# Projecting out the third unit by seven block products, in a fused RWKV-6 and MoE kernel

## The chip, the cores and the metric

The kernel runs on one core of a Trainium2 chip. The metric is the device time of one launch in microseconds (us). Five engines run side by side, each with its own queue of instructions that it works off in order: TensorE (matrix products; PE in the profile, PEld its weight loads), VectorE (DVE), ScalarE (ACT), GpSimd (POOL) and SyncE (SP, which issues most DMAs). They meet only through semaphores.

## What is computed

Two parts follow each other. First a linear attention with a state that decays (RWKV-6), over 4 batches, 8 heads, 768 tokens, heads of 48. Then a feed-forward layer over the 3072 tokens, from 384 to 2048 and back, in float32:

```python
for t in range(S):
    cur = np.einsum('bhd,bhe->bhde', u[None] * kt, vt)
    y[:, :, t] = np.einsum('bhd,bhde->bhe', rt, state + cur)
    state = wt[:, :, :, None] * state + np.einsum('bhd,bhe->bhde', kt, vt)
...
h = x @ w_in
sp = np.maximum(h, 0.0) + np.log1p(np.exp(-np.abs(h)))
g = h * erf(sp)
return (g @ w_out).astype(np.float32)
```

## The kernel before, in words

**Units and steps.** The 3072 tokens are cut into 12 units of 256 tokens (two batches of 128 tokens, `UNIT`), numbered from 0. Step s computes the attention of unit s. Behind it, and interleaved by hand on the same engines, step s computes the hidden layer of unit s-1 (`hidden`, eight pieces, each two rows of 128 of the 2048) and the projection back of unit s-3 (`project` or `project_fast`). `n_steps` is 12, `DIRECT` is 4. Steps 1 to 4 run `attend`, steps 5 to 11 `attend_late`. "The third unit" is unit 2, which is projected out in step 5; "the fifth step" is step 4.

**The hidden layer.** A piece (the token H) is twelve instructions on TensorE at L1097 into one of two PSUM buffers `m`, which ScalarE copies to `h` (L1106). Units 0 to 2 (below `FAST`) get their activation through `activate`: two halves of 2048 elements a partition, each a softplus (L1079), an error function (L1082) and two multiplies (L1086), called one after another by `advance`, the token A. From unit 3 on the hidden layer is cut into four chunks of 1024 elements: `softplus_chunk` (s, L1053) writes one shared stretch of `room`, `erf_chunk` (ey or ep, L1057) writes its result into a "lane" in PSUM, either the bank of `y` or the second bank of products, and `multiply_chunk` (m, L1062) multiplies `h` by it on VectorE. Softplus and error function need different tables, so ScalarE loads a table ahead of each.

**The projection.** `project` (L1114) makes the two output tiles of a unit from 32 products of 384 columns (L1129, 64 instructions, since a float32 product is two), in eight pieces (the token P), and ScalarE copies each tile out (L1138). `project_fast` (L1197) treats the product as 2 x 2 blocks and takes seven block products of 8 x 192 columns instead of eight, in Strassen's manner as Winograd arranged it; it is used from unit 3 on. Each P is one block product:

```python
product(m0[:, lo], a11, b11, True)      # then o[0] low half <- m0, L1218
product(m1[:, lo], a22, t4, True)
product(m1[:, hi], s1, t1, False)       # then o[1] <- m1, L1223
product(m0[:, lo], s2, t2, False)       # then o[0] high half <- m0, L1226
product(m1[:, hi], s4, b22, False)
product(m0[:, lo], s3, t3, False)       # then o[1] += m0 (L1232), DMA out
product(m1[:, lo], a12, b21, True)      # then o[0] += m1 (L1237), DMA out
```

It needs four sums of blocks of the activations: `blend` makes them on VectorE, tokens S1 (L1189), S2 (L1191), S3 (L1193), S4 (L1195), into `room[1]` to `room[3]` and, for S3, in place. In the later steps, blocks of `h` are first copied to a PSUM lane by ScalarE (`to_lane`, the tokens k22y, k11p, k12y, L1170). It also needs four differences of the weights (`mix_weights`, L1153): three are made on VectorE in step 3, and the last, which overwrites a block of `w_out_sb` that the plain projection still reads, on GpSimd by the token G.

**The order.** `attend` in step 4 calls `in_order` at five places, and `attend_late` calls `run_late` at seven ("front", "near", 0 to 4). Both read a string of tokens; F is the next part of the preparation of the following step's attention. Step 5 has strings of its own (`LATE[DIRECT + 1]`), steps 6 to 10 take `USUAL`. At the last two places of step 4, between the two strings, stand the transposes and the state products of the attention (L1010, L734), the update of the middle state and the next state (L1031, L1034, L1035), and the rest of step 5's preparation (L333, L589); behind the last one come the products through the state (L685), the copies of `y` and `xT` (L693, L714) and six small DMAs for xT (L720), three of them issued by ScalarE. The first place of step 5 follows the products of level 5 (L627) and VectorE's L333 and L637.

Of the kernel before, what the change touches and what calls it, by code (L numbers as in the profile page):

```python
# [16 lines left out]

P = 128
FAST = 3
EP = 64  # L20
HC = 64
NC = 2
# [17 lines left out]
DIRECT = 4  # L40
# [21 lines left out]
def kernel(  # L62
# [26 lines left out]
    SPC = NB // NJ  # L89
    assert C == P == NC * HC and HC == 1 << LOG and NE == 2 and D <= EP and NP * NE * D == DM == KT * P  # L90
    assert n_steps == SPC * n_pairs and NP == KT + 1 == 4 and NG == 2 and P // NEAR * NH == P
# [214 lines left out]
    def rows(e, n=D):  # L306
        return slice(e * EP, e * EP + n)

    both = slice(0, EP + D)

# [362 lines left out]
    def through_state(s, xT):  # L673
# [42 lines left out]
        for kk in range(KT):  # L716
            n = D // KT
            for e in range(NE):
                queue = nc.scalar if (kk, e) in by_scalar else nc.sync
                queue.dma_start(  # L720
                    out=xT[e * EP + D : (e + 1) * EP, kk, :],
                    in_=y3[e * EP + kk * n : e * EP + (kk + 1) * n, :],
                )
# [18 lines left out]
    def spread_blocks(s, pp):  # L742
# [3 lines left out]
        for e in range(NE):  # L746
            nc.tensor.matmul(
                pp[:EP, e, 0:2, HC // 2 : HC // 2 + n],
                lhsT=over_blocks[rows(e)].rearrange("p b n -> p (b n)"),
# [302 lines left out]
    def softplus_chunk():  # L1052
        nc.scalar.activation(sp_room, chunks[0], AF.Softplus)  # L1053

    def erf_chunk(kind):
        at = lane(kind).rearrange("p (f t) -> p f t", t=UNIT)
        nc.scalar.activation(at, sp_room, AF.Erf)  # L1057
        started.append((chunks.pop(0), at))

    def multiply_chunk():  # L1060
        h, at = started.pop(0)
        nc.vector.tensor_mul(h, h, at)  # L1062

    def hidden(of, xT, gs, cut):


        def activate(h):

            held = []

            def softplus():
                n = 2 * (rooms["next"] % 2)
                rooms["next"] += 1
                held.append(
                    room[:, n : n + 2].rearrange("p i n -> p (i n)").rearrange(
                        "p (f t) -> p f t", t=UNIT
                    )
                )
                nc.scalar.activation(held[0], h[:], AF.Softplus)  # L1079

            def erf():
                nc.scalar.activation(held[0], held[0], AF.Erf)  # L1082

            def multiply():
                for part in (slice(0, FG // 2), slice(FG // 2, FG)):
                    nc.vector.tensor_mul(h[:, part], h[:, part], held[0][:, part])  # L1086

            later.extend([(softplus, True), (erf, True), (multiply, False)])

        for g in range(NG):  # L1090
            h = hid.tile([P, FG, UNIT], FP32, name="h")
            gs.append(h)
            for f in range(0, FG, FT):
                ps = ps_m.tile([P, FT, UNIT], FP32, name="m")
                for ff in range(FT):
                    for kk in range(KT):
                        nc.tensor.matmul(  # L1097
                            ps[:, ff, :],
                            lhsT=w_in_sb[:, g * FG + f + ff, kk * P : (kk + 1) * P],
                            rhs=xT[:, kk, :],  # L1100
                            start=kk == 0,
                            stop=kk == KT - 1,
                        )
                    if cut and not ff and g == NG - 1 and f == FG - FT:
                        yield
                nc.scalar.copy(h[:, f : f + FT, :], ps[:])  # L1106
                if of >= FAST:
                    if f % (2 * FT):
                        chunks.append(h[:, f - FT : f + FT])
                elif f == FG - FT:  # L1110
                    activate(h)
                yield
# [48 lines left out]
    blends, lanes = {}, {}  # L1161
# [6 lines left out]
    def to_lane(of, what, kind):  # L1168
        lanes[what] = lane(kind).rearrange("p (f t) -> p f t", t=C)
        nc.scalar.copy(lanes[what], quarter(of, what))  # L1170
# [96 lines left out]
    def join_tokens():  # L1267

        made = ins.tile([P, 2, JP, C], FP32, name="in")
        made = made[:].rearrange("p x n t -> p (x n t)").rearrange("p (i t) -> p i t", t=UNIT)  # L1270
        t1, t2, t3, t4, less = (made[:, i] for i in range(5))
        one, two = ([xTs[of][:, kk, :] for kk in range(KT)] for of in (n_steps - 2, n_steps - 1))
        for out_, a, b in (
            (t1, two[0], one[0]), (t2, two[1], t1), (t4, one[1], t2), (less, one[2], two[2]),
            (t3, two[1], two[0]),
        ):
            nc.vector.tensor_sub(out_, a, b)
        turns["joint tokens"] = one, two, t1, t2, t3, t4, less
# [62 lines left out]
    def activate_pair(what):  # L1341

        if what == "u":
            h = chunks.pop(0)
            i, k = divmod(slots["next"] % 4, 2)
            slots["next"] += 1
            n = FT * UNIT
            at = room[:, i, k * n : (k + 1) * n].rearrange("p (f t) -> p f t", t=UNIT)
            nc.scalar.activation(at, h, AF.Softplus)
            slots["u"].append((h, at))  # L1350
        elif what == "v":
            h, at = slots["u"].pop(0)
            nc.scalar.activation(at, at, AF.Erf)
            slots["v"].append((h, at))
        else:
            h, at = slots["v"].pop(0)
            nc.vector.tensor_mul(h, h, at)

    xTs, hids, projs = {}, {}, {}
    gated = [[] for _ in range(n_steps)]  # L1360

    def advance(count=None):

        while later and count != 0:
            stage, last = later.pop(0)
            stage()
            count = count and count - 1
            if last and not count:
                break
# [10 lines left out]
    def piece(kind, of):  # L1380
        if not 0 <= of < n_steps:
            return
        if of not in kind:
            if kind is hids:
                kind[of] = hidden(of, xTs[of], gated[of], not of)
            else:
                kind[of] = (project_fast if of >= FAST else project)(of, gated[of])
        next(kind[of])

    def in_order(s, k):  # L1390


        order = ("APPP", "APPP", "APPHH", "AHHH", "AHHH")
        for what in order[k]:
            if what == "A":
                advance()
            elif what == "P":
                piece(projs, s - 3)
            else:
                piece(hids, s - 1)  # L1400


    STAGES_LATE = ("front", "near", 0, 1, 2, 3, 4)
    LATE = {
        DIRECT + 1: (
            "s ey", "m", "s ep m P P s ey m P P P", "s P F ep m P F P k22y k11p F", "S1",
            "S2 S3 H k12y S4 H F", "s H ep m H H F G s H H H ep",
        ),
        n_steps - 1: (
            "s P", "m w", "ey P m s P P ep P", "m P P", "", "", ""  # L1410
        ),
# [6 lines left out]
    def run_late(s, tokens, following=None):  # L1418

        for what in tokens.split():  # L1420
            if what == "A":
                advance()
            elif what == "P":
                piece(projs, s - 3)
            elif what == "H":
                piece(hids, s - 1)
            elif what == "F":
                next(following, None)
            elif what == "Q":
                piece(projs, s - 2)  # L1430
            elif what == "J":
                next(turns["joint"])
            elif what == "w":
                next(joining)
            elif what in "uvz":
                activate_pair(what)
            elif what == "T":
                join_tokens()
                turns["joint"] = hidden_of_two()
            elif what == "G":  # L1440
                mixing.send(nc.gpsimd)
            elif what == "s":
                softplus_chunk()
            elif what[0] == "e":
                erf_chunk(what[1])
            elif what == "m":
                multiply_chunk()
            elif what[0] == "k":
                to_lane(s - 2, what[1:3], what[3])
            else:  # L1450
                blend(s - 2, *(int(n) for n in what[1:]))
                if what == "S3":
                    del lanes["11"], lanes["22"]
                elif what == "S4":
                    del lanes["12"]

    CONVERT = (
        (),
# [21 lines left out]
    for kk in range(KT):  # L1480
        n = D // KT
        to, of = (x.rearrange("p (e m) -> p e m", e=NE) for x in (apart[:, kk], ident[:]))
        nc.vector.tensor_copy(out=to[:, :, D:], in_=of[:, :, kk * n : (kk + 1) * n])
    load_first()
    with tc.manual_schedule(
# [15 lines left out]
        for s in range(n_steps):  # L1501
# [7 lines left out]
            def place(n):  # L1509
# [4 lines left out]
                if s >= DIRECT:  # L1514
                    in_order(s, next(places))
                    return
# [43 lines left out]
        s = n_steps  # L1560
# [108 lines left out]
```

## Time and profile before

| | us |
|---|---|
| median of 3 runs (lowest, highest) | 581.49 (580.64, 581.67) |
| the profiled execution, its time | 581.53 |
| its span, first to last instruction | 579.7 |

The profile is of one execution. Its span leaves out what lies before the first and after the last instruction. The granted TensorE clock is 1.00 throughout. Busy time of each engine in the steps around the change, all us:

| step | from, to | length | TensorE | VectorE | ScalarE | GpSimd |
|---|---|---|---|---|---|---|
| 4 | 143.83, 192.54 | 48.71 | 48.71 | 35.10 | 21.59 | 36.01 |
| 5 | 192.54, 237.16 | 44.62 | 44.62 | 38.14 | 35.53 | 28.66 |
| 6 | 237.16, 281.46 | 44.30 | 44.30 | 37.42 | 31.44 | 22.93 |
| 7 | 281.46, 325.76 | 44.30 | 44.30 | 37.42 | 29.24 | 22.94 |

A line of the timeline reads: start, length, engine, line of the kernel, operation, output <- input, shape, how many; in brackets the idle time of the engine ahead of it and what ended that.

### The profile page before, as it was taken

Reading aid. Unit: us, or ns where it says so; the run is one execution under the profiler, and the core shown is the slowest. Engines: PE = TensorE matmul, PEld = TensorE weight load, DVE = VectorE, ACT = ScalarE, POOL = GpSimd, SP = SyncE. Lnnn points to the kernel's source line nnn. Section 1 sums busy time; section 2 is a strip of 40 time slices with the busy share of each in tenths; the row PEclk is TensorE's granted clock in tenths of the full one; section 3 lists DMA queues with packets and bytes.
Section 4 is the critical chain, followed back from the end, with each engine's and each line's share of the span. In section 5 each row is a group of like instructions: output and inputs, shape, how many; then the busy total and the mean of one; then the engine's idle time right before and its main releaser. Section 6 shows DMA issues by size and latency. Waiting matters only on the chain.

```text
span 579.7 us, 16499 instructions
## 1 busy us (share of the span) xinstructions
PE 572.8 (99%) x7240; PEld 492.2 (85%) x7240; DVE 429.0 (74%) x462; ACT 354.8 (61%) x478; POOL 244.8 (42%) x264
## 2 busy tenths in 40 slices
PE   8999999999999999999999999999999999999997
PEld 6678887688578668998998998898898899988997
DVE  7775876998894789699599599599599527256640
ACT  3658777545444698756766766766666661388700
POOL 3557391604793885284185175176174000000000
PEclk9999999999999999999999999999999999999999
DMA  7695662350453314245235236234232201000000
GB/s 261 190 325 233 235 207 83 148 161 2 145 151 98 107 44 169 41 139 177 41 125 192 39 124 193 39 111 163 47 110 83 47 8 37 1 1 2 28 27 28
DMA packets 54081, 63.24 MB, mean 109 GB/s; under 512 B 35160, under 2 KB 40568, under 8 KB 52984
## 3 DMA queue, kind: packets, MB, share of 16 engines
q1 hardware_dynamic: 53624, 61.98, 33.8%
q8 instruction: 57, 0.93, 0.7%
q10 hardware_dynamic: 384, 0.20, 0.1%
q14 instruction: 16, 0.13, 0.1%
HBM read 52.39 MB, written 8.69 MB: 105 GB/s over the span
## 4 chain that ended last, share of the span: by engine, by line
PE 95%; DVE 1%; POOL 1%; DMA 1%; issue 1%; ACT 0%; SPq 0%; DVEq 0%; POOLq 0%; ACTq 0%
PE m L1097 35%; PE m L1212 28%; PE m L1129 11%; PE pp L627 5%; PE pp L1300 4%; PE y L1300 2%; PE y L659 2%; PE y L685 2%; PE pp L734 2%; PE m L934 1%; DMA words<-in_moe_w_in 1%; PE pp L943 1%; PE pp L1010 1%; POOL tot_sb L355 0%; PE pp L1212 0%
## 5 line engine op out<-in xcount | busy, mean ns | idle before, releaser
L1097 PE MATMUL m<-xT,w_in_sb 128*128 128x256 f32 x960 | 214.8, 382 | 0.4 <-ACT h L1106 0.3
L1097 PEld LDWEIGHTS m<-xT,w_in_sb 128*128 128x128 f32 x960 | 180.1, 190 | 25.8 <-issue 0.5
L333 DVE TENSOR_TENSOR in<-in,tot_sb 128x1024 f32<-128x1024 f32 (+1 forms) x55 | 76.4, 1389 | 16.9 <-PE pp L627 15.5
L1106 ACT COPY h<-m 128x512 f32<-128x512 f32 x80 | 46.3, 579 | 59.7 <-PE m L1097 59.7
L1129 PE MATMUL m<-w_out_sb,h 128*128 128x384 f32 x192 | 64.3, 491 | 0.0
L1129 PEld LDWEIGHTS m<-w_out_sb,h 128*128 128x128 f32 x192 | 35.8, 190 | 23.4
L1212 PE MATMUL m<-mixed,h 128*128 128x192 f32 x256 | 45.6, 332 | 0.0
L1212 PE MATMUL m<-w_out_sb,h 128*128 128x192 f32 x256 | 44.8, 329 | 0.0
L1212 PEld LDWEIGHTS m<-mixed,h 128*128 128x128 f32 x256 | 41.4, 190 | 0.9
L1057 ACT ACT_TABLE_LOAD x30 | 38.5, 1283 | 5.9 <-DVE h L1062 5.4
L1212 PEld LDWEIGHTS m<-w_out_sb,h 128*128 128x128 f32 x256 | 41.6, 190 | 0.3
L1212 PE MATMUL m<-w_out_sb,room 128*128 128x192 f32 x240 | 41.5, 326 | 0.0
L1053 ACT ACT_TABLE_LOAD x30 | 38.5, 1283 | 3.2 <-issue 2.7
L462 POOL TENSOR_TENSOR words<-words,own 128x384 f32<-128x384 f32 x21 | 30.7, 1462 | 22.8 <-DVE words L493 13.1
L627 PEld LDWEIGHTS pp<-in 48*48 48x48 f32 (+4 forms) x2368 | 30.1, 120 | 11.8 <-issue 6.2
L503 POOL TENSOR_TENSOR words<-words 128x384 f32<-128x384 f32 x28 | 39.7, 1447 | 0.0
L1212 PEld LDWEIGHTS m<-w_out_sb,room 128*128 128x128 f32 x240 | 39.4, 190 | 0.0
L455 POOL TENSOR_TENSOR own<-rest 128x384 f32<-128x384 f32 x7 | 9.8, 1396 | 60.8 <-ACT o L1218 49.8
L627 PE MATMUL pp<-in 48*48 48x32 f32 (+4 forms) x2368 | 34.0, 206 | 0.2 <-DVE in L333 0.2
L503 POOL TENSOR_TENSOR rk<-words 128x384 f32<-128x384 f32 x28 | 32.4, 1186 | 0.0
L528 DVE TENSOR_REDUCE sums<-rk 128x16 f32<-128x768 f32 (+2 forms) x31 | 31.6, 1021 | 0.0
L1053 ACT ACTIVATE room<-h 128x1024 f32<-128x1024 f32 x28 | 29.6, 1057 | 0.3
(204 smaller groups left out, 980.0 us busy)
## 6 DMA issues: line engine op xcount, KB each, us to landing
in<-in_rkw SPq DMA_DIRECT2D x8, 1024.0 KB, 5.1
words<-in_moe_w_in SPq DMA_DIRECT2D x16, 384.0 KB, 5.3
words<-in_moe_w_out SPq DMA_DIRECT2D x16, 384.0 KB, 5.5
words<-in_rk_rows SPq DMA_DIRECT2D x8, 768.0 KB, 5.7
w<-in_rkw SPq DMA_DIRECT2D x11, 512.0 KB
v<-in_v SPq DMA_DIRECT2D x12, 384.0 KB, 5.5
out<-o SPq DMA_DIRECT2D x23, 192.0 KB, 3.1
in<-in_rkw SPq DMA_DIRECT2D x7, 512.0 KB, 6.0
```

Source lines behind the costliest of these rows:

```text
L333: nc.vector.tensor_mul(halves, halves, view(tots[level - 1], 0, [[1, n], [2, nb], [0, half]]))
L462: engine.tensor_mul(to, to, of[:, :, None, :].to_broadcast([P, NEAR // 2 // half, half, D]))
L503: engine.tensor_mul(to[:, i], r[:, half:], k[:, part * rows + i, None].to_broadcast([P, half, D]),)
L528: nc.vector.tensor_reduce(out=to, in_=of, axis=mybir.AxisListType.X, op=ALU.add)
L627: nc.tensor.matmul(to, lhsT=rk(1, n)[rows(e), s0 : s0 + m], rhs=right, start=True, stop=True,)
L1053: nc.scalar.activation(sp_room, chunks[0], AF.Softplus)
L1057: nc.scalar.activation(at, sp_room, AF.Erf)
L1097: nc.tensor.matmul(ps[:, ff, :], lhsT=w_in_sb[:, g * FG + f + ff, kk * P : (kk + 1) * P], rhs=xT[:, kk, :], start=kk == 0, stop=kk == KT - 1,)
L1106: nc.scalar.copy(h[:, f : f + FT, :], ps[:])
L1129: nc.tensor.matmul(ps[j][:], lhsT=gs[g][:, f, j * C : (j + 1) * C], rhs=w_out_sb[:, g * FG + f, :], start=g + f == 0, stop=g == NG - 1 and ...
L1212: nc.tensor.matmul(to, lhsT=a[:, f], rhs=b[:, f], start=start and f == 0, stop=f == FG - 1, skip_group_check=True,)
L1300: nc.tensor.matmul(to[:, e], lhsT=a[:, 2 * i + e], rhs=b, start=start and not k, stop=True, skip_group_check=True,)
```

## The change

Unit 2 too is projected out by `project_fast`. So its four sums are now made in step 4, where the last weight difference (G) moves as well, and both of unit 2's remaining activation stages run at the fourth of the five places. The first two chunks of unit 3 get their softplus and error function in step 4 (and the first its multiply). Step 5 loses its own order and takes `USUAL`, with seven P instead of eight, chunks 2 and 3 of unit 3 at its start and chunks 0 and 1 of unit 4 at its end. Unit 2's blocks are summed straight from `h`, with no copies to a lane, so the names of lanes are dropped only if they are there.

```diff
+SEVEN = 2
...
-                kind[of] = (project_fast if of >= FAST else project)(of, gated[of])
+                kind[of] = (project_fast if of >= SEVEN else project)(of, gated[of])
...
-        order = ("APPP", "APPP", "APPHH", "AHHH", "AHHH")
-        for what in order[k]:
-            if what == "A":
-                advance()
-            elif what == "P":
-                piece(projs, s - 3)
-            else:
-                piece(hids, s - 1)
+        order = (
+            "A P P P", "A P P P", "A P P H H", "A A S1 S2 G H H s H", "ep H s H m S4 S3 ep H",
+        )
+        run_late(s, order[k])
...
     LATE = {
-        DIRECT + 1: (
-            "s ey", "m", "s ep m P P s ey m P P P", "s P F ep m P F P k22y k11p F", "S1",
-            "S2 S3 H k12y S4 H F", "s H ep m H H F G s H H H ep",
-        ),
...
-                if what == "S3":
-                    del lanes["11"], lanes["22"]
-                elif what == "S4":
-                    del lanes["12"]
+                for name in {"S3": ("11", "22"), "S4": ("12",)}.get(what, ()):
+                    lanes.pop(name, None)
```

The order that step 5 now takes is the one that stands in the code for steps 6 to 10:

```python
USUAL = (
    "s P", "m", "ey P m s P P ep P", "m k22y P F P k11p F F", "S1", "S2 S3 H k12y S4 H F",
    "s H ey m H H F s H ep H H",
)
```

## The prediction

> **What bounds the kernel now.** I read the page's busy shares first, then its chain of waits by engine, then the same chain in order of time, to see which steps hold the edited products and whether TensorE ever waits there.
>
> ```profile
> PE 572.8 (99%) x7240; PEld 492.2 (85%) x7240; DVE 429.0 (74%) x462; ACT 354.8 (61%) x478; POOL 244.8 (42%) x264
> ...
> PE 95%; DVE 1%; POOL 1%; DMA 1%; issue 1%; ACT 0%; SPq 0%; DVEq 0%; POOLq 0%; ACTq 0%
> ```
>
> TensorE is both the busiest engine and 95% of the chain. In steps 4 to 6 the chain is unbroken TensorE (start, length, what):
>
> ```profile
> 193.25 13.10 PE m L1129 x40
> 206.35 0.69 PE pp L627 x50
> 207.28 7.94 PE m L1129 x24
> 215.22 0.86 PE pp L734 x64
> 216.08 21.08 PE m L1097 x96
> ...
> 238.46 2.80 PE m L1212 x16
> 241.26 0.59 PE y L659 x32
> 241.85 0.90 PE y L685 x64
> 242.75 10.60 PE m L1212 x64
> 253.34 0.69 PE pp L627 x50
> 254.28 5.40 PE m L1212 x32
> 259.68 0.86 PE pp L734 x64
> 260.54 20.92 PE m L1097 x96
> ```
>
> Step 5 begins at 192.54, step 6 at 237.16. The reader is to see that each piece starts where the one before ends (one gap of 0.24 us at 207.04), that the plain projection (L1129) sits in step 5 and that step 6 already runs the seven-product form (L1212). So what TensorE saves is worth its full length, until some other engine makes it wait. Which one can is read from ScalarE's and VectorE's order of time in those steps.
>
> **The change part by part.**
>
> *Removed and added on TensorE.* Unit 2's plain projection is 13.10 + 7.94 = 21.04 us (64 instructions of 384 columns). The seven products of unit 3 in step 6 are 2.80 + 10.60 + 5.40 = 18.80 us (112 of 192 columns). Unit 2's operands have the same shapes and places, so I take that: **-2.24 us**. The first of seven products (P1) takes 2.80 us, the next four 2.65 each, the last two 2.70 each; the hidden pieces (H, L1097) take 20.92 / 8 = 2.615 each.
>
> *Sums of unit 2 (S1, S2, S3, S4; new, four VectorE additions of 128x1024) and the last multiply (L1086) a stage earlier.* An addition with all operands in SBUF is 1.22 us (rows of L1195 in the later steps: 1.21 to 1.23), the pair of L1086 2.35. In the fourth place of step 4 VectorE now idles 6.51 us before L1031:
>
> ```profile
> 169.46 3.95 DVE L1086 TENSOR_TENSOR h<-h,room 128x1024 f32<-128x1024 f32 x2
> ...
> 183.25 0.55 DVE L1031 TENSOR_TENSOR middle<-faded,pp 112x384 f32<-112x384 f32 x1 [6.51 <-PE pp L734]
> ...
> 193.32 1.23 DVE L333 TENSOR_TENSOR in<-in,tot_sb 128x1024 f32<-128x1024 f32 x1 [3.47 <-PE pp L627]
> ```
>
> ScalarE's second error function there ends at 178.51. From it the pair and S1, S2 run to 178.6 + 2.35 + 2 x 1.15 = 183.3 (neighbours overlap by some 0.07), where L1031 starts anyway. TensorE needs `middle` only at about 192. In the fifth place the pair (2.35) leaves and m, S4, S3 (three of 1.15) come: VectorE ends about 191.1 instead of 189.85, before its next work at 193.32. **Cost 0**, covered by those two idle stretches; if the cover were gone, what is late next is that L333 of step 5 and everything behind it.
>
> *The token G* (the last weight difference, L1153 on GpSimd, 3.46 us at 223.14 in step 5) moves to step 4, where GpSimd is free from 175.08 (end of L1017) to 183.88. Its input columns are last read by unit 1's projection, which ends at 167.65. Cost 0. If something held it past 178.6 it would lie beside the pair and S1, S2, and a pair beside GpSimd's work took 3.95 instead of 2.35, so 0.8 more per addition; that would still be under the 2.2 us that VectorE has at 191.1.
>
> *Four activations moved* (softplus and error function of unit 3's chunks 0 and 1) onto ScalarE in step 4. Each is a table load of 1.28 and 1.03 to 1.06 of work, and the copies that free the two buffers of H (L1106) queue behind them. Playing it with the rows of step 4: the error function of unit 2 ends at 178.51 and the copies of two H follow at 178.4 and 179.67, as now; then softplus to 182.6, the third copy to 183.1 instead of 182.85; error function to 185.4; copy at 186.36 as now; softplus to 189.3; copy to 189.85; error function to 192.1 (it also waits for m, which frees the PSUM lane, 188.8); last copy to 192.65 instead of 192.12. An H needs the copy of the H two before it: the fourth place's third starts at 179.63 against 179.0, the others have 2 us and more. So no wait, and the copy of `y` (192.61 now) is at most 0.1 late. **Cost 0.**
>
> The Trainium skill speaks against this part: "ScalarE: Activation LUTs", section "What ACT_TABLE_LOAD costs", puts a drain of about 1380 ns behind each load, 2.66 us a switch. By that figure ScalarE would be some 5.5 us later by the end of step 4 and the sum would be a loss. The trace doesn't bear it out:
>
> ```profile
> 196.48 1.28 ACT L1053 ACT_TABLE_LOAD   x1 [2.67 <-issue]
> 197.78 1.06 ACT L1053 ACTIVATE room<-h 128x1024 f32<-128x1024 f32 x1
> 198.85 1.28 ACT L1057 ACT_TABLE_LOAD   x1
> ```
>
> Load, work and next load follow within 0.02 us: a switch costs 1.28 here.
>
> *Step 5 takes the usual order* with chunks 2 and 3 only. ScalarE has 12 switches there now and 8 after; VectorE has four m ahead of S1 now and three after (1.15 less), and gets L1232 and L1237 (2 x 0.54 by step 6's rows). SP's queue: the two output DMAs still stand ahead of step 5's loads of rows and w, and are issued no later (214.71 now). New on TensorE's side are two waits.
>
> First, the fifth product (P5) overwrites what L1223 copies, so it waits for ScalarE. In step 5 nothing stands between P1 and P5 on TensorE, while step 6 has 0.59 + 0.90 us of attention there: P1 to P4 run from 193.25 to 193.25 + 2.80 + 3 x 2.65 = 204.00. ScalarE's first switch is at 196.48, since it issues three DMAs for xT before. In step 6 the same stretch runs from 240.14 to the end of L1223 at 249.09, 1.31 of it copies of y and xT that step 5 has earlier: 8.95 - 1.31 = 7.64, so 204.12. Queued behind P5 is all of TensorE. I take **+0.2** (0.12 and some signalling). Bounds: after step 3's end the way from the y copy to the first switch was 143.90 to 146.71, 1.06 shorter than in step 5 (192.61 to 196.48), which gives 0; as much longer gives 1.2.
>
> Second, in the H phase TensorE comes nearer to VectorE than in step 6. VectorE front to front is 193.32 against 238.54, and its step-5 chain to the first m is 0.3 longer (12.67 against 12.36). So L1232 ends at 258.99 - 45.22 + 0.3 = 214.1; TensorE reaches the first H, which needs that buffer, at 204.2 + 2.65 + 0.94 + 5.40 + 0.86 = 214.05. Just met. The copies behind S1 and the lane copy (L1170) follow VectorE: the fourth H's copy ends at 272.58 - 45.22 + 0.3 = 227.7, the sixth H could start at 214.1 + 5 x 2.615 = 227.2. I take **+0.3** (0 to 1.0: step 6 has 1.0 to 1.5 in hand at these places, step 5 is 1.5 us tighter).
>
> **Sum:** -2.24 + 0.2 + 0.3 = -1.74 us. From step 6 on VectorE waits for TensorE once a step (seen L668, up to 3.5 us; L333), so the shift is kept to the end. Span 579.7 - 1.74 = 577.96. The profiled run's time was 581.53 and its span 579.7; the median of the runs is 581.49, 1.79 above the span. **Forecast 579.75 us**, 0.3% faster.
>
> **Rivals.**
>
> 1. *The gain is mostly eaten by the two new waits* (1.0 or more together): 579.7 - 1.2 or less, 580.3 to 581.5, about 580.8. For it: no slack at P5, the first H and the sixth H by the working above; ScalarE's DMA issue in step 5 was irregular (0.53, then 2.54 for two). Against: the waits share slack, a wait at P5 relieves the H phase.
>
> 2. *VectorE becomes the bound of step 5* (the other side). Place: from the erf at 178.51 to L333 at 193.32. Eight operations with two SBUF operands now stand there beside up to 7 us of GpSimd work (G, L1034, L407). If each is slowed as the pair at 169.46 was (3.95 against 2.35, 0.8 each), VectorE is 6.4 late, 4.2 after its 2.2 of slack; the first H then waits 4.0 for L1232, and step 5 loses 4.0 + 0.2 - 2.24 = 2 us: 583.5. It decides from 2.2 us of delay, and turns the sign from some 4.4. For it: L407 took 5.95 at 184.80 beside VectorE and 1.05 at 226.56 alone. Against: in that same stretch it was GpSimd that waited, VectorE kept 1.22 an operation.
>
> 3. *A table switch costs more where copies of H are mixed in*, say a second 1.28 each. Four switches in step 4 make ScalarE 5.1 us late at P5, which has nothing in hand: 5.1 + 0.5 - 2.24 = +3.4, so 584.9. Against: in step 5, copies and switches are mixed from 223.39 on (L1053, L1106, L1057) and nothing lies between them. The page on ScalarE in the Trainium skill, named above, would have it so, with 1.38 in place of my 1.28.
>
> 4. *The step gives all of it and the gaps too* (0.24 at 207.04, 21.08 against 20.92 in the H phase): -2.24 - 0.4 = 578.85.
>
> 5. *The seven products don't replace the eight*, no change: nothing in the order or operands allows it.
>
> **How the numbers follow.** Forecast (waits 0 to 1.0, 579.2 to 580.3) 0.69, rival 1 0.17, rival 2 0.10, rival 3 0.01, rival 4 0.03, rival 5 below 0.01. What a measurement of this kernel can tell from no change is 0.2%, 1.16 us. Faster by more: 0.69 + 0.03 = 0.72. Within: rival 1, 0.17. Slower: 0.11. The range goes from rival 4 (578.8) over the forecast's own 579.2 to 580.3 up to where the gain is wholly eaten (581.5).
>
> **What would show it.** In the changed profile step 5 should have seven L1212 products of 18.8 us in all from the same start (within 0.2 of 193.25); TensorE gaps before the fifth product and in the H phase of 0.5 us together; G on GpSimd near 175 at 3.5 us; L1031 within 0.5 of 183.3; step 6 starting about 1.7 us earlier and every later step 44.3 long. I am wrong if TensorE waits over 1 us in step 4, if L333 of step 5 starts late, or if L1223 ends after 205.

## The result, and the profile after

The changed kernel's median is 579.48 us (578.2 to 581.45, 22 runs) against 581.12 us (579.7 to 583.53, 22 runs) for the kernel before, measured together. The ratio is 0.9972, with a 95% interval of 0.996 to 0.9983: 0.28% faster, 1.6 us. The forecast was 0.3%, 1.74 us. The profiled execution's span is 577.8 us (forecast 577.96). Line numbers of the changed kernel, in the lines quoted below, are one higher than before.

The page's busy shares and its chain by engine:

```profile
PE 570.1 (99%) x7288; PEld 497.2 (86%) x7288; DVE 435.1 (75%) x468; ACT 355.2 (61%) x479; POOL 244.3 (42%) x264
...
PE 95%; DMA 2%; ACT 1%; DVE 1%; SPq 0%; issue 0%; DVEq 0%; ACTq 0%
```

TensorE is still the bound: it is busy 2.7 us less, with 48 more instructions. VectorE took on 6.1 us (the four sums, and the two additions at L1233 and L1238). Of the 2.7, 0.84 lies in the first 50 us (46.29 to 45.45), with the same number of instructions, ahead of every edit; it isn't the change's. What the change brought is in the chain in order of time (start, length, what; step 5 and the head of step 6):

```profile
192.36 0.70 PE pp L628 x64
193.06 13.42 PE m L1213 x80
206.48 0.69 PE pp L628 x50
207.17 0.25 PE pp L748 x4
207.42 5.40 PE m L1213 x32
212.81 0.86 PE pp L735 x64
213.68 21.52 PE m L1098 x96
235.20 0.59 PE y L660 x32
...
240.79 10.60 PE m L1213 x64
```

The seven products take 13.42 + 5.40 = 18.82 us in the place of 21.04, and the H phase 21.52 in the place of 21.08. Between the starts of those rows step 5 is 42.84 us long, before it was 44.62: -2.22 + 0.44 = -1.78. The rest of the difference of the two spans, 0.18 us, is there at the start of step 5 (192.36 against 192.54) and, 0.19, at that of step 4 (143.64 against 143.83), ahead of every edit, so it is no gain of the change. The 1.96 at the start of step 6 is kept to the end of the chain.

The short row L748 also mends a reading of mine: the 0.24 us ahead of 207.28 that I called a gap in the kernel before is this work (L747 there), which the shortened chain had left out.

The two waits that were forecast can be seen at the weight loads of TensorE, the first line for the fifth product, the others for the H phase, which is the eight hidden pieces one behind the other (in brackets the idle time ahead and what ended it):

```profile
203.61 2.57 PEld L1213 LDWEIGHTS m<-w_out_sb,room 128*128 128x128 f32 x16 [0.25 <-ACT o L1224]
...
213.61 7.63 PEld L1098 LDWEIGHTS m<-xT,w_in_sb 128*128 128x128 f32 x36
221.46 2.46 PEld L1098 LDWEIGHTS m<-xT,w_in_sb 128*128 128x128 f32 x12 [0.21 <-ACT h L1107]
224.31 2.46 PEld L1098 LDWEIGHTS m<-xT,w_in_sb 128*128 128x128 f32 x12 [0.39 <-ACT h L1107]
227.16 7.64 PEld L1098 LDWEIGHTS m<-xT,w_in_sb 128*128 128x128 f32 x36 [0.40 <-ACT h L1107]
```

The fifth product waited 0.12 us for L1224: its first instruction starts 2.72 us after the fourth product's, where 2.60 is usual. The fourth, fifth and sixth H each wait for ScalarE's copy of the H two before. The idle time of a weight load is longer than the wait of its product, since it starts ahead of it (195.53 against 195.69 for the second product): the H phase is 0.60 longer than the 20.92 of the later steps, not 1.00.

ScalarE's order of time says why those copies are late:

```profile
216.50 0.59 ACT L1107 COPY h<-m 128x512 f32<-128x512 f32 x1 [1.45 <-PE m L1098]
219.88 1.02 ACT L1171 COPY y<-h 128x1024 f32<-128x1024 f32 x1 [2.78 <-DVE room L1190]
220.83 0.58 ACT L1107 COPY h<-m 128x512 f32<-128x512 f32 x1
```

The second H is done at 218.9 (213.68 + 2 x 2.615), but its copy stands behind the lane copy k12y, which waits 2.78 us for VectorE's S1. Table loads, softplus and error function follow, and each later copy is late by the same.

Step 4 took the sums, the activations and G without a wait of TensorE. VectorE there:

```profile
178.36 2.36 DVE L1087 TENSOR_TENSOR h<-h,room 128x1024 f32<-128x1024 f32 x2 [1.79 <-ACT room L1083]
180.75 1.23 DVE L1190 TENSOR_TENSOR room<-h 128x1024 f32<-128x1024 f32 x1
182.01 1.23 DVE L1192 TENSOR_TENSOR room<-room,h 128x1024 f32<-128x1024 f32 x1
183.16 0.55 DVE L1032 TENSOR_TENSOR middle<-faded,pp 112x384 f32<-112x384 f32 x1
...
188.52 1.62 DVE L1196 TENSOR_TENSOR room<-h,room 128x1024 f32<-128x1024 f32 x1
190.07 1.42 DVE L1194 TENSOR_TENSOR h<-h 128x1024 f32<-128x1024 f32 x1
193.13 1.50 DVE L334 TENSOR_TENSOR in<-in,tot_sb 128x1024 f32<-128x1024 f32 x1 [1.65 <-PE pp L628]
```

L1032 starts where it did (183.16, before 183.25), right behind S2, and 1.65 of the 3.47 us of idle time ahead of L334 are left. G ran on GpSimd from 174.86 for 3.45 us.

### The profile page after: what moved, and what is told of

Same layout as the page of the kernel before. It is cut to its first block, busy times and chain, and to the rows that moved or that the text cites. A ratio compares the mean times of both kernels' runs of the same rounds, so it can differ in the third digit from the quotient of the medians.

```text
span 577.8 us, 16604 instructions
## 1 busy us (share of the span) xinstructions
PE 570.1 (99%) x7288; PEld 497.2 (86%) x7288; DVE 435.1 (75%) x468; ACT 355.2 (61%) x479; POOL 244.3 (42%) x264
## 4 chain that ended last, share of the span: by engine, by line
PE 95%; DMA 2%; ACT 1%; DVE 1%; SPq 0%; issue 0%; DVEq 0%; ACTq 0%
PE m L1098 35%; PE m L1213 32%; PE m L1130 7%; PE pp L628 5%; PE pp L1301 4%; PE y L1301 2%; PE y L660 2%; PE y L686 2%; PE pp L735 2%; DMA words<-in_moe_w_in 1%; PE pp L944 1%; PE pp L1011 1%; DMA u_sb<-in_u 1%; PE pp L1213 0%; PE m L935 0%; SPq L151 0%
## 5 line engine op out<-in xcount | busy, mean ns | idle before, releaser
L334 DVE TENSOR_TENSOR in<-in,tot_sb 128x1024 f32<-128x1024 f32 (+1 forms) x55 | 77.4, 1407 | 15.7 <-PE pp L628 14.3
L1213 PE MATMUL m<-mixed,h 128*128 128x192 f32 x288 | 51.2, 331 | 0.0
L1213 PE MATMUL m<-w_out_sb,h 128*128 128x192 f32 x288 | 50.4, 329 | 0.0
L1213 PEld LDWEIGHTS m<-mixed,h 128*128 128x128 f32 x288 | 46.6, 190 | 1.0
L1213 PEld LDWEIGHTS m<-w_out_sb,h 128*128 128x128 f32 x288 | 46.8, 190 | 0.4
L1213 PE MATMUL m<-w_out_sb,room 128*128 128x192 f32 x272 | 47.1, 326 | 0.0
L1213 PEld LDWEIGHTS m<-w_out_sb,room 128*128 128x128 f32 x272 | 44.6, 190 | 0.3 <-ACT o L1224 0.3
L1130 PE MATMUL m<-w_out_sb,h 128*128 128x384 f32 x128 | 43.2, 492 | 0.0
L628 PEld LDWEIGHTS pp<-in 48*48 48x48 f32 (+4 forms) x2368 | 30.1, 120 | 12.3 <-issue 7.3
L1130 PEld LDWEIGHTS m<-w_out_sb,h 128*128 128x128 f32 x128 | 23.7, 190 | 15.4
L456 POOL TENSOR_TENSOR own<-rest 128x384 f32<-128x384 f32 x7 | 10.0, 1432 | 61.5 <-ACT o L1219 61.5
L628 PE MATMUL pp<-in 48*48 48x32 f32 (+4 forms) x2368 | 33.9, 206 | 1.1 <-DVE in L334 1.1
```

The source lines that it names most:

```text
L334: nc.vector.tensor_mul(halves, halves, view(tots[level - 1], 0, [[1, n], [2, nb], [0, half]]))
L628: nc.tensor.matmul(to, lhsT=rk(1, n)[rows(e), s0 : s0 + m], rhs=right, start=True, stop=True,)
L1130: nc.tensor.matmul(ps[j][:], lhsT=gs[g][:, f, j * C : (j + 1) * C], rhs=w_out_sb[:, g * FG + f, :], start=g + f == 0, stop=g == NG - 1 and ...
L1213: nc.tensor.matmul(to, lhsT=a[:, f], rhs=b[:, f], start=start and f == 0, stop=f == FG - 1, skip_group_check=True,)
```

## The experiments

Each is an edit of the changed kernel. "Step 5" is measured from the start of L628 in it to the start of step 6's first L660, in the engine's order of time, in each kernel's own profile (0.1 us above the length by the chain's rows; the expectations mix the two). A time marked as one run can be 1 or 2 us off, as the spread above shows, so the verdict is read from the step. Ratios are to the kernel before as it ran beside each: its median was 581.12 beside the changed kernel, 581.24 beside `both` and the repeat, 581.56 beside `reorder_only`, `products_only`, `no_k12` and `s1_ahead`, and 580.83, one run, beside the last three.

| kernel | step 5, us | H phase, us | median, us | ratio to before (95%) |
|---|---|---|---|---|
| before | 44.73 | 21.15 | 581.12 | 1 |
| changed | 42.95 | 21.59 | 579.48 | 0.9972 (0.996 to 0.9983) |
| changed, again | 42.95 | 21.47 | 579.94 | 0.9976 (0.9957 to 0.9996) |
| reorder_only | 44.56 | 20.99 | 581.0 | 0.9989 (0.9974 to 1.0003) |
| products_only | 48.91 | | 585.72, one run | |
| no_k12 | 42.32 | 20.99 | 578.99 | 0.996 (0.9944 to 0.9977) |
| s1_ahead | 42.36 | 20.99 | 579.39 | 0.9959 (0.9939 to 0.9979) |
| both | 42.32 | 20.99 | 579.52 | 0.9969 (0.995 to 0.9987) |
| two_more | 44.53 | 21.61 | 580.57, one run | |
| five_more | 50.18 | 24.02 | 585.76, one run | |
| late_g | 45.28 | 21.61 | 582.99, one run | |

**Is it the products or the order?** `reorder_only` keeps the moved chunks and the usual order of step 5, with the eight plain products:

```diff
-SEVEN = 2
+SEVEN = 3
-"A A S1 S2 G H H s H", "ep H s H m S4 S3 ep H"
+"A A H H s H", "ep H s H m ep H"
+DIRECT + 1: ("s P", "m", "ey P m s P P ep P", "m k22y P F P P k11p F F", "S1",
+             "S2 S3 H k12y S4 H F", "s H ey m H H F G s H ep H H"),
```

> Unit 2 is projected out by the eight plain products again, without its four sums; the two chunks of unit 3 stay moved into step 4 and step 5 keeps the usual order. Theory (the gain is TensorE's shorter projection): step 5 as long as in the kernel before, 44.4 to 44.7 us, plain projection 21.04 us, time within 0.1% of before. Rival (the order with the chunks moved ahead brought the gain): step 5 shorter than 44.0 us and the time at least 0.15% below before.

Step 5 is 44.56 us, 0.17 less than before, nearly all of it in the H phase (20.99 for 21.15). The ratio's point, 0.9989, is 0.1% below 1, and its interval holds 1. So by the profiles some 0.17 of the 1.78 us could come from the order alone, and the rest needs the products.

**Can the products go without the order?** `products_only` leaves unit 3's first chunks in step 5:

```diff
-"A A S1 S2 G H H s H", "ep H s H m S4 S3 ep H"
+"A A S1 S2 G H H H", "H H S4 S3 H"
+DIRECT + 1: ("P s ey", "m", "P P P P s ep m s ey m", "s P F ep m P F k22y k11p F", "S1",
+             "S2 S3 H k12y S4 H F", "s H ep m H H F s H H H ep"),
```

> Seven products and the sums in step 4 as in the change, but unit 3's first two chunks stay in step 5, which so has 12 table switches on ScalarE (order: P s ey, m, P P P P s ep m s ey m, ...). Theory (ScalarE's order, not its idle time, decides): the state products wait for the copies behind the third chunk by some 2 us and the H phase for the lane copies by 2 to 3; step 5 is 47 to 49 us and the time 582 to 584. Rival (the 9 us that ScalarE idles in step 5 take the switches up): step 5 under 43.5 us and the time as in the changed kernel.

Step 5 came out at 48.91, inside the expected 47 to 49; the time that I had worked out beside it, 582 to 584, was too low by my own step (44.73 to 48.91 is 4.2 us, and 581.56 + 4.2 = 585.7). TensorE's order of time:

```profile
214.88 0.94 PE L735 MATMUL pp<-v,kT 64*48 64x48 f32 x64 [2.11 <-ACT own L645]
215.98 2.86 PE L1098 MATMUL m<-xT,w_in_sb 128*128 128x256 f32 x12 [0.17 <-DVE o L1233]
221.30 4.05 PE L1098 MATMUL m<-xT,w_in_sb 128*128 128x256 f32 x10 [2.47 <-DVE o L1238]
```

The state products wait for ScalarE's copies behind the third chunk, as expected; the second wait is for VectorE's L1238, which stands behind a chunk's multiply that waits for ScalarE. Of the 6.0 us that step 5 is longer than in the changed kernel, some 1.6 are no wait: from 221.3 to 224.3 TensorE's granted clock is 0.50, and the 84 instructions behind the last wait take 20.02 us, where 84 of the later steps' take 18.3 (20.92 / 96 each). So the move of the chunks brings next to nothing by itself, but in this order the seven products would have cost 4 us without it. Another placing of the four chunks in step 5 was not tried.

**What the 0.44 us of the H phase are.** Two edits of step 5 alone, each by a different way:

```diff
 no_k12:   "S2 S3 H k12y S4 H F"  ->  "S2 S3 H S4 H F"
 s1_ahead: "m k22y P F P k11p F F", "S1"  ->  "m k22y P F P k11p F", "S1 F"
```

> The changed kernel, but in step 5 the copy of the block 12 to a PSUM lane (k12y) is left out and S4 reads it from h. Theory (the waits of the hidden pieces in step 5 come from ScalarE standing at k12y, which waits for VectorE's S1, while the copy of the second H stands behind it): the H phase of step 5 falls from 21.52 to 20.9 to 21.1 us, step 5 to about 42.3, some 0.5 us below the changed kernel. Rival (ScalarE is simply too full there with table switches): the H phase stays above 21.3.

> The changed kernel, but in step 5 S1 goes ahead of the third F (a scaling of 1.7 us on VectorE that the next step needs). Theory: S1 starts near 216.9 instead of 218.63, k12y 1.7 earlier, the copy of the second H in time, and the H phase falls to 20.9 to 21.1 us; about 0.5 us below the changed kernel, as without k12y. Rival (ScalarE too full, or the scaling is missed later): the H phase above 21.3, or a new VectorE wait of the same size after it.

In both the H phase falls to 20.99 us, the 20.92 of the chain's rows in steps 6 and later, and step 5 to 42.3. ScalarE in `no_k12`:

```profile
215.60 0.58 ACT L1107 COPY h<-m 128x512 f32<-128x512 f32 x1 [1.42 <-PE m L1098]
218.19 0.58 ACT L1107 COPY h<-m 128x512 f32<-128x512 f32 x1 [2.00 <-PE m L1098]
218.80 1.28 ACT L1054 ACT_TABLE_LOAD   x1
```

Now the second copy waits for TensorE, not TensorE for it. The table switches behind it are the same as in the changed kernel, so a full ScalarE wasn't the cause; its place in a queue was. In `s1_ahead` S1 started 23.69 us after the first product instead of 25.64, and the scaling put behind it made nothing late. `both` and a repeat of the changed kernel were run on one chip:

> The changed kernel without k12y in step 5 and with S1 ahead of the third F there. Theory (each alone has already taken every wait of the H phase away, and the rest of step 5 is TensorE's own work): step 5 42.3 us, as with either alone, no further gain; ratio to before 0.995 to 0.997, some 0.001 below the changed kernel. Rival (both still leave waits of their own that add): step 5 under 42.2 us.

> The changed kernel as it is, to stand on the same chip beside the combined version. Step 5 again 42.9 to 43.0 us with an H phase of 21.5; ratio to before 0.996 to 0.998.

Step 5 is 42.32 again, no further gain. A wait of 0.2 us or less is left in each: ahead of the first H, for L1233, in `both` (the weight load idle for 0.24), ahead of the fifth product, for L1224, in the two others (0.19 and 0.26); the rest is TensorE's own work. The versions without the waits of the H phase are 0.6 us shorter in step 5, and their ratios to the kernel before lie below the changed kernel's by 0.0007 to 0.0013, but the intervals overlap, and only `both` ran beside the changed kernel: the step shows the gain, the timing alone doesn't prove it.

**Where the cover ends.** `two_more` and `five_more` make S4 again two and five times in step 4 (same values), so that VectorE is late for step 5:

```diff
-"ep H s H m S4 S3 ep H"
+"ep H s H m S4 S4 S4 S3 ep H"            (two_more; five_more has S4 six times)
```

> The changed kernel with S4 made three times in step 4 (2.3 to 2.5 us more on VectorE, same values). Theory (1.65 us of cover is left ahead of L334 in step 5, and behind it VectorE meets the first H with none in hand): step 5 grows by 0.5 to 0.9 us, to about 43.5. Rival (VectorE's chain in step 5 has room of its own): no change, 42.8.

> The changed kernel with S4 made six times in step 4 (5.7 to 6.5 us more on VectorE, same values). Theory: VectorE is 4 to 5 us late at L334 in step 5, the first H waits as long for L1233, step 5 is 46.5 to 47.7 us long, and the kernel is 1.5 to 3 us slower than before the change. Rival (room further on): step 5 under 45 us.

Both grew step 5 by more than expected, 1.58 and 7.23 us. In `two_more` L334 started 0.84 us after the first product instead of 0.14, so 0.70 late, but L1233 22.11 us after it instead of 20.53 (by end), 1.58 late. VectorE between:

```profile
195.01 1.48 DVE L535 TENSOR_TENSOR rk<-words,u_row 128x768 f32<-128x768 f32 x1
196.42 1.35 DVE L485 TENSOR_TENSOR rk<-words 128x384 f32<-128x384 f32 x1
```

In the changed kernel they took 1.14 and 0.54. GpSimd's L408 had been kept waiting by the additions, so that its L789 and L456 moved from 192.71 and 193.51 to 194.84 and 195.64 and now lay beside these two; that this is what slowed them is read from the overlap, no run tests it alone. In `five_more` VectorE was 4.46 us late at L334 and 4.8 at L1233, as expected, and TensorE waited 2.56 us ahead of the state products and 2.31 ahead of the first H. That is 4.9; the other 2.4 is in the H phase, 24.02 against 21.59, though the 0.60 of waits for ScalarE's copies that the 21.59 holds is gone. Its windows (TensorE busy, weight loads, VectorE, ScalarE, GpSimd, granted clock, DMA share, GB/s):

```profile
211.00:214.10 3.10, 0.54 (x4) 0.24 (x3) 3.10 (x3) 3.02 (x5) 3.10 (x3) 1.00 0.00 0
214.10:217.30 3.20, 0.94 (x64) 0.81 (x64) 3.20 (x5) 0.44 (x1) 3.20 (x4) 0.91 0.21 63
217.30:220.00 2.70, 2.65 (x6) 2.19 (x7) 2.70 (x3) 1.52 (x2) 2.62 (x3) 0.50 0.46 164
220.00:223.00 3.00, 3.00 (x8) 2.36 (x7) 2.96 (x3) 0.12 (x1) 1.39 (x1) 0.50 0.78 228
```

After the two waits TensorE's granted clock is 0.50 from the first H on, for some 6 us; 14 instructions fill 5.7 us, the time of 26 at 0.216 us each.

**G without its cover.** `late_g` moves G behind L1035:

```diff
-"A A S1 S2 G H H s H", "ep H s H m S4 S3 ep H"
+"A A S1 S2 H H s H", "ep H s H m G S4 S3 ep H"
```

> The changed kernel with G moved one place later in step 4, behind L1035, beside S4 and S3. Theory (G costs nothing only because GpSimd and VectorE are idle from 175 to 178.4): G takes 6 us or more there, GpSimd's totals and its L463 in step 5 come 3 us late, VectorE's L488 waits for them, and step 5 grows by 1.5 to 3 us, to 44.3 to 45.8. Rival (GpSimd has room): step 5 within 0.3 us of 42.84.

Step 5 is 45.28, as expected, but by the other engine. G kept its time, and VectorE paid (G is L1154 on GpSimd):

```profile
185.66 3.44 POOL L1154 TENSOR_TENSOR w_out_sb<-w_out_sb 128x1536 f32<-128x1536 f32 x1
```

```profile
186.21 3.98 DVE L334 TENSOR_TENSOR in<-in,tot_sb 128x1024 f32<-128x1024 f32 x1
190.10 2.06 DVE L590 TENSOR_TENSOR own<-block_sb,by_tokens 128x1024 f32<-128x1024 f32 x1
```

Both are 1.22 in the changed kernel, so VectorE loses 3.6 us, the larger part beside G and the rest beside GpSimd's next operation, L408 (from 189.05). The multiply m that frees the lane comes late, then ScalarE's second error function, then L1224: the fifth product waits 1.72 (by the starts of the two products) instead of 0.12, and the first H 0.62 for L1233.

## Why the prediction was right

- **The saving on TensorE, -2.24.** Measured: 21.04 to 18.82, -2.22, with the wait of 0.12 inside it. Without the wait the products are 18.70, 0.10 shorter than unit 3's in step 6: there attention work stands between the first and the second product, and the product behind it takes 0.1 longer (2.70 by the starts, where 2.60 is usual). `reorder_only` shows that it is this term that makes the gain.
- **The wait of the fifth product, +0.2.** 0.12, the size that I had worked out, but in part by luck. L1224 ended at 203.56, 0.56 ahead of my 204.12: ScalarE's first switch was as much ahead (195.92 instead of 196.48), 0.18 of it by the earlier start of the step. From there to its end it took 7.64, as forecast. TensorE was ready at 203.50 by the starts in its order of time, 0.50 ahead of my 204.00, since P1 to P4 take 10.51 and not 10.75 us, and the step began earlier. The two misses cancel.
- **The H phase, +0.3.** +0.44 against before, 0.60 against the later steps. The place (the copies behind k12y behind S1) was right and is shown by `no_k12` and `s1_ahead`; the size was half of what came. My own working gave 0.5 for the sixth H (227.7 against 227.2), and I took 0.3. And I set the whole wait against the kernel before, whose H phase already held 0.16 of waiting, so that 0.60 of wait is 0.44 of loss.
- **The sum.** -2.34 for the products, +0.12 and +0.44 make -1.78, the forecast was -2.24 + 0.2 + 0.3 = -1.74. The terms are right in kind; that the sum is within 0.04 is luck, since one miss of 0.18 and one of 0.14 go opposite ways. The measured medians, 1.64 apart with an interval of 1.0 to 2.3, can't tell such differences.
- **The sums, the moved activations and G in step 4, 0.** Right: no wait of TensorE in step 4 or at the front of step 5. Two additions took 1.62 and 1.42 instead of 1.22, beside GpSimd's L408, which cost 0.6 of VectorE's cover and nothing else. (Of the rows of L1195 that I took the 1.22 from, most have one operand in PSUM; the first two sums here, with all operands in SBUF, took 1.23.) ScalarE's copy of `y` started at 192.42, right behind the products through the state, which end at 192.36.
- **Table switches.** They still cost 1.28 us each and the next instruction followed within 0.02; the rival with a dearer switch is out. The drain that the Trainium skill puts behind a load doesn't show in any of these rows.
- **VectorE as the bound.** It didn't happen, with 1.65 us to spare. The price that I gave that rival was too low: I had 4.0 us of wait for 4.2 of lateness, where 4.46 cost 7.23 in `five_more`, since TensorE's granted clock fell after the waits there, and, as `two_more` shows, a late VectorE can meet GpSimd at other places. The point from which it decides, 2.2 us, was nearer to 1.65.
- **The reading of the gap** at 207.04 was wrong, as shown above, so half of the fourth rival's extra 0.4 us never existed.

## What to carry to other kernels

When one engine is the whole chain, a change that shortens its work is worth that length only as long as the others keep up, and the place where they stop keeping up can be worked out from a steady step of the kernel as it is, instruction by instruction, by sliding one engine's row against another's. Work that is "hidden" needs its cover named with a number: here 3.5 us of idle VectorE of which 1.65 were left, and one weight difference a place later (+2.3 us) would have eaten the whole gain, and two additions more (+1.6) nearly all of it. A small wait that remains is worth looking at for what stands ahead of the late instruction in its queue: one copy left out, or one addition put ahead of a scaling, took it away.

## What the runs showed of the hardware that I had not expected

**Waits can cost clock.** In `five_more`, two waits of TensorE of 2.56 and 2.31 us, with only 0.94 us of small products between them, were followed by a granted clock of 0.50 for some 6 us of the H phase, which took 24.02 us instead of the 20.99 that it takes without waits: another 3.0. In `products_only`, waits of 2.11 and 2.47 us were followed by 0.50 too, for some 3 us, though 0.94 us of small products and 2.86 us of a hidden piece lay between. In `late_g`, waits of 1.56 and 0.62 left it at 1.00. The Trainium skill ("TensorE: Matmul & The Clock Gate", "Part 1: The HAM clock gate") lets the clock fall after an idle window of about 3.4 us; no wait here is that long alone, but the products between didn't hold the clock up. How long a wait may be isn't settled by these runs: in `s1_ahead`, near the start of the kernel and far from its edit, the clock was 0.50 from 31 to 34 us behind idle times of which the longest in the 10 us before was 1.53.

**Either engine can be the one that pays.** In the kernel before, L407 on GpSimd took 5.95 us beside VectorE's operations on two SBUF inputs (1.05 at 226.56 alone), while VectorE kept its 1.22:

```profile
184.80 5.95 POOL L407 TENSOR_TENSOR tot_sb<-w 128x512 f32<-128x512 f32 x1
...
185.22 1.22 DVE L333 TENSOR_TENSOR in<-in,tot_sb 128x1024 f32<-128x1024 f32 x1
```

In `late_g`, G started 0.55 us ahead of VectorE's L334, kept its 3.44 us, and L334 took 3.98. The Trainium skill ("SBUF — State Buffer", "Who interferes with whom") says that the two engines share a port pair, and that the order of issue decides who blocks. The rows of `late_g` agree. Those of the kernel before don't by their starts, since L407 began 0.42 us ahead of L333 and yet paid; why stays open. My estimate of G's lateness, 6 us or more, had put the loss on the wrong engine.
